# Due times of attention in a fused attention and two-MLP kernel: a weight conversion step moved behind an evacuation, and other places moved by tenths

## The chip, the cores and the metric

The kernel runs on one core of a Trainium2 chip. The metric is the device time of one execution in microseconds, the median of several runs. Engines are called as the profile does: PE (TensorE), DVE (VectorE), ACT (ScalarE), POOL (GpSimd), SP (SyncE, which issues the DMAs).

## The reference, cut to what matters

Attention over 2 x 8 heads, 768 positions and 64 features per head, with a mask from locality-sensitive hashing; then an MLP with a sigmoid gate; then an MLP with a quadratic activation.

```python
def _attn_ref(q, k, v, proj):
    q_bits = (np.einsum('bhsd,dk->bhsk', q, proj) > 0).astype(np.int64)
    ...
    mask = q_bucket[:, :, :, None] == k_bucket[:, :, None, :]
    scores = scale * np.matmul(q, k.transpose(0, 1, 3, 2))
    scores = np.where(mask, scores, -1000000000.0)
    scores = scores - np.max(scores, axis=-1, keepdims=True)
    attn = np.exp(scores)
    attn = attn / (np.sum(attn, axis=-1, keepdims=True) + 1e-09)
    return np.matmul(attn, v).astype(np.float32)

def _moe_ref(x, w_gate, w_val, w_out):
    gate = 1.0 / (1.0 + np.exp(-(x @ w_gate)))
    val = x @ w_val
    return (gate * val @ w_out).astype(np.float32)

def _moe2_ref(x, w_in, w_out):
    h = x @ w_in
    g = np.where(h >= 1.0, h, np.where(h <= -1.0, 0.0, (h + 1.0) ** 2 / 4.0))
    return (g @ w_out).astype(np.float32)
```

The MLP weights come as 64-bit floats; 1536 tokens of 512 features pass through both MLPs.

## The kernel before

**Attention** works on eight pairs of heads, numbered 0 to 7 by the loop variable q. A pair has twelve units (six blocks of 128 rows for each of the two heads). For a unit, TensorE makes the scores (QK, line 597) in one of two PSUM score buffers, VectorE takes the row maximum (MAX, 605), ScalarE the exponential with its row sum (EXP, 609). The results are transposed in eighteen groups of 512 columns for each pair: TensorE transposes (T, 631), ScalarE writes a scaled half-precision copy (HI, 640), VectorE the rest that the copy lost (LO, 643); three PSUM banks (p0, p1, mm) serve the transposes in the order in which they come free. Three products with the values follow in each pair (PV, 709), all in one PSUM bank with the tag "pv" and one buffer, each cut into three runs of twelve steps. VectorE evacuates a product with one instruction (EV, line 718), which multiplies it with the inverse row sums. Those arrive over GpSimd (RB, 890), TensorE (R, 875) and ScalarE (RS, 879). In this text T 7.17 is the transpose with index 17 of pair 7, and E7.1 is the evacuation with index 1 of pair 7, that of attention's last but one product; E7.2 is the last one.

**Weights.** The MLP weights are 64-bit floats, which the kernel takes apart into 32-bit words and rebuilds as 32-bit floats: the absolute value of the high words (a_abs, ScalarE, 164), the largest one over both halves (a_max, VectorE, 265 and 267), then a_conv in six steps: clamping (step 0, GpSimd, 167), a shift (1, VectorE, 170), the low words of half 0 and half 1 (2 and 3, line 173), and the sign of half 0 and half 1 (4 and 5, line 176). Four sums of quarters follow (a_sum, line 334; the first adds two quarters of half 1), since the first MLP's products are made by a scheme with fewer multiplications (the products a, b, c, d, e of class Quad), and scaled copies and rests (a_hi 342, a_lo 350). The scale comes from the row of maxima (row_in, 239 to 249) over a DMA. "g0" and "v0" are the first chunks of gate and value weights, "g1" the next chunk of gate weights; a chunk's two raw buffers are loaded on SyncE's queue (a_load, 309 to 312) when an older chunk's conversion has left them.

**What sets the order.** Every operation of attention has a due time: 12 times the pair, plus a number from a table (AT for the first and last pair, AM for those between, F0 for special steps of pair 0). The list of operations is sorted by due time and written out in that order (line 1030), so that a number in a table decides only what stands before what on each engine's queue. The conversion of v0 is placed by line 1024, the g0 steps by line 977. The program of the MLPs is a second list of that kind (line 1581), and some of its instructions stand, in the queues, between the last ones of attention. Lines 1032 to 1048, without due times, finish attention and the first gate product. The second MLP ends with strips of products (class Quad2), whose first strip takes its places from PA[0].

Of the kernel before, what the change touches and what calls it, by code (L numbers as in the profile page):

```python
# [23 lines left out]
EXP = 0x7F800000  # L24
# [12 lines left out]
def lsh_attention_glu_act(ctx, tc, qt, kt, v, proj, w_gate, w_val, w_out1, w_in2, w_out2, ident_d, code_d, out):  # L37
# [435 lines left out]
    with ExitStack() as actx:  # L473
# [246 lines left out]
        NAT, PR, VR, VS, RS, PT, STS = {}, {}, {}, {}, {}, {}, {}  # L720
# [7 lines left out]
        with tc.manual_schedule():  # L728
# [54 lines left out]
            for dst, r in ((3, E), (2, O)):  # L783
# [8 lines left out]
            F0 = {  # L792
                "max": (0.835, 4.3363, 4.8113, 6.0),
                "first": (1.1116, 1.92, 2.6321, 2.6521),
# [5 lines left out]
                "MAX": (-0.86, 0.21, 0.88, 1.91, 2.7, 4.3082, 4.6882, 5.3482, 7.3656, 9.7482, 9.8482, 8.9617),  # L800
                "EXP": (0.22, 0.6565, 1.1565, 2.5865, 2.8165, 4.4, 4.86, 7.05, 8.14, 10.5074, 11.21, 9.27),
# [9 lines left out]
                "BITS": (3.6634,),  # L811
# [13 lines left out]
            AM = {  # L825
                "QK": (-1.6212, -0.312, 0.1234, 1.0922, 0.2911, 4.4841, 2.6311, 3.1388, 4.9681, 7.5662, 8.3203, 9.8239),
                "MAX": (-0.8384, -0.282, 0.274, 2.0221, 1.7029, 4.7833, 2.832, 3.457, 5.7284, 8.6318, 8.8402, 9.9223),
                "EXP": (-0.0169, 0.1389, 0.7054, 2.7327, 1.7202, 5.1256, 3.1579, 4.9368, 7.4948, 9.0696, 9.801, 10.9635),
# [17 lines left out]
                "V4": (8.2939,),  # L846
                "RB": (7.5895, 9.9185, 12.8309),
                "VR": (7.1203,),
                "VT": (10.3243,),
                "STP": (6.1912, 6.7323, 11.461),  # L850
            }
# [8 lines left out]
            def at(kind, i, q, fn, *args):  # L860
                prog.append((UP * q + (tab(q)[kind][i] if isinstance(kind, str) else kind), len(prog), fn, args))
# [43 lines left out]
            for q in range(NQ):  # L905
# [46 lines left out]
                if q + 1 < NQ:  # L952
                    T = tab(q)
# [22 lines left out]
            for i in range(13):  # L976
                q, t = ((1, 1.3756), (1, 2.5756), (1, 5.1058), (2, 2.7058), (2, 3.9058), (2, 5.1058), (2, 6.3058), (3, 2.9841), (3, 7.7841), (4, 2.7841), (4, 4.7739), (4, 5.3408), (4, 6.0))[i]
                at(t, 0, q, next, fw, None)
            last = NQ - 1
# [41 lines left out]
            for i in range(2):  # L1021
                at(11.9 + 0.65 * i, 0, last, a_abs, "v0", i)
                at(10.8628 + 0.7012 * i, 0, last, a_max, "v0", i)
            for i, t in enumerate((13.0012, 13.3012, 13.6012, 13.4, 13.85, 14.0)):
                at(t, 0, last, a_conv, "v0", i)
# [391 lines left out]
    for m in range(2):  # L1417
# [3 lines left out]
        "g": {"seed": (0.4974, 2.358, 4.976), "p5": 3.5377, "sum": (3.99, 5.128, 7.1683, 8.1683), "act": (5.4565, 7.5607, 8.0579, 7.094)},  # L1421
        "v": {"seed": (0.3623, 2.8959, 5.4602), "p5": 2.4313, "sum": (3.0782, 5.7535, 7.5389, 6.9122), "act": (3.7144, 5.3665, 5.5617, 6.5916)},
    }
# [5 lines left out]
    for k in range(1, 2 * NT):  # L1429
        s0, T = 7 * k, QP[name(k // 2)[0]]  # L1430
# [8 lines left out]
    for t in range(2, NT):  # L1439
        base, n = 14 * (t - 1), name(t)  # L1440
        T = WP[n if n in WP else n[0]]
# [102 lines left out]
    ZA = [z_at((1.5403, 2), (3.2361, 2), (6.5761, 4), (11.2361, 2), (13.0358, 2)), z_at((1.3658, 2), (4.6958, 4), (9.3658, 3), (14.1405, 3))]  # L1544
    PA = [(2.33, -0.4877, 4.1823, 5.0776, 8.8423, 9.8423, 12.67), (1.0, -1.7115, 3.33, 4.306, 8.0, 9.0, 12.0)]
    SA = [(3.367, 8.2105, 11.95), (2.01, 6.95, 10.6)]
    CA = [{"a": (6.3682, 7.0823, 7.5823, 8.7823, 10.1657), "b": (10.8729, 11.3823, 11.9323, 13.0675, 13.3852), "c": (12.5147, 12.9147, 12.9295, 15.0221, 16.7088), "d": (13.55, 14.2829, 14.8829, 15.4829, 15.5329)},
          {"a": (5.34, 5.8, 6.3, 7.4, 7.9), "b": (9.6, 10.5884, 10.9383, 12.2, 12.8), "c": (11.1, 11.6, 12.2, 12.75, 13.8127), "d": (13.9575, 14.4775, 14.9497, 15.4997, 15.9997)}]
    for w in range(F2H + 1):
# [5 lines left out]
        if w == F2H:  # L1555
            break
        for i, d in enumerate(PA[m]):
            on(t0 + d, m_op, w, "P", i)
# [3 lines left out]
        for i, g in ((4, "b"), (5, "c")):  # L1562
            on(t0 + PA[m][i] + 1.0537, m_op, w, "add", g)
        for g, ds in CA[m].items():
# [64 lines left out]
```

## Time and profile before

| | us |
| --- | --- |
| median of 3 runs | 761.7 |
| lowest, highest run | 761.12, 762.7 |
| profiled execution | 759.33 |
| its span, first to last instruction | 757.5 |

Lengths and starts in the rows below belong to the profiled execution, counted from the start of its span. Attention takes up about the first 240 us of it. In a timeline, a row gives the start, the length, the engine, the source line, the operation, what it writes and reads, and in brackets the idle time before it with the operation that ended it. Several instructions of a kind that follow one another are one row (x2, x12).

### The profile page before, as it was taken

To read this page: it belongs to the slowest core of one execution; us is meant where nothing else is said; L and a number is where in the kernel's file an instruction comes from. 1 tells how busy PE (TensorE), PEld (TensorE's weight loads), DVE (VectorE), ACT (ScalarE), POOL (GpSimd) and SP (SyncE) were. 2 spreads that over 40 slices of the span, in tenths; PEclk is the share of its full clock that TensorE was granted. 3 is DMA by queue.
4 is the path that set the end of the run, shared out by engine and by line. 5 is a ranking of instruction groups with operands and counts; after the bars stand their busy time and mean duration, and the time that the engine had idled before them with its cause. 6 is when DMAs were issued, how large, how long until landed. Compare 5 with 4: busy or idle time off the path is not lost.

```text
span 757.5 us, 13220 instructions
## 1 busy us (share of the span) xinstructions
PE 728.7 (96%) x4883; PEld 461.5 (61%) x4883; DVE 648.1 (86%) x1141; ACT 521.1 (69%) x985; POOL 227.5 (30%) x311
## 2 busy tenths in 40 slices
PE   7899999999998999998999999998999999999997
PEld 4778878888885555555555556664555555555553
DVE  6899999889888989998889999999999996766643
ACT  6789889988885674673764445546776677767753
POOL 6435267774685653463430001103000000000000
PEclk9999999999999999999999999999999999999999
DMA  8564554454302155556565913533333200100002
GB/s 253 157 184 113 137 146 121 106 128 100 100 1 56 57 180 197 178 170 209 180 230 199 406 56 112 168 112 113 110 112 94 73 1 29 57 0 1 1 1 83
DMA packets 53200, 89.59 MB, mean 118 GB/s; under 512 B 9872, under 2 KB 33040, under 8 KB 53136
## 3 DMA queue, kind: packets, MB, share of 16 engines
q1 hardware_dynamic: 52400, 88.07, 37.8%
q8 instruction: 38, 0.62, 0.3%
q10 hardware_dynamic: 736, 0.69, 0.3%
q14 instruction: 26, 0.21, 0.1%
HBM read 68.65 MB, written 3.15 MB: 95 GB/s over the span
## 4 chain that ended last, share of the span: by engine, by line
PE 35%; DVE 22%; DMA 4%; ACT 3%; issue 2%; POOL 1%; SPq 1%; ACTq 0%; DVEq 0%; POOLq 0%
DVE h L131 2%; PE p L423 2%; PE p L422 2%; PE p L421 2%; DMA gi<-in_moe_w_in_dram 2%; PE qa L1357 2%; DVE gmx L209 2%; PE qa L1356 2%; PE qa L1355 2%; PE qe L1356 2%; PE qe L1355 2%; PE qe L1357 2%; PE o L1356 2%; PE o L1357 2%; PE o L1355 2%; DVE h L392 2%
## 5 line engine op out<-in xcount | busy, mean ns | idle before, releaser
L643 DVE SCALAR_TENSOR_TENSOR PT<-pt,PT 128x512 f16<-128x512 f32 x144 | 95.2, 681 | 8.5 <-ACT PT L640 7.0
L605 DVE TENSOR_REDUCE st<-sc 128x1 f32<-128x768 f32 x96 | 90.7, 948 | 6.5 <-PE sc L597 5.5
L609 ACT ACTIVATE P<-sc,st 128x768 f32<-128x768 f32 x96 | 87.1, 908 | 8.7 <-DVE st L605 7.9
L640 ACT ACTIVATE PT<-pt 128x512 f16<-128x512 f32 x144 | 82.2, 599 | 11.4 <-PE pt L631 9.7
L631 PE MATMUL pt<-ident,P 128*128 128x128 f32 x576 | 80.9, 279 | 0.8 <-DVE PT L643 0.5
L631 PEld LDWEIGHTS pt<-ident,P 128*128 128x128 f32 x576 | 65.4, 142 | 13.7 <-issue 8.8
L709 PE MATMUL O<-PT,vh 128*64 128x256 f16 x576 | 54.4, 277 | 2.1 <-DVE xr L718 2.1
L421 PE MATMUL p<-y,i 128*128 128x384 f16 x128 | 41.7, 326 | 0.0
L422 PE MATMUL p<-y,i 128*128 128x384 f16 x128 | 41.7, 326 | 0.0
L423 PE MATMUL p<-y,i 128*128 128x384 f16 x128 | 41.7, 326 | 0.0
L709 PEld LDWEIGHTS <-vh 128*64 128x64 f16 x576 | 31.0, 109 | 15.1 <-issue 14.6
L1357 PEld LDWEIGHTS <-g 128*128 128x128 f16 x192 | 18.9, 98 | 25.1 <-DVE g L131 2.3
L709 PE MATMUL O<-PT,vl 128*64 128x256 f16 x288 | 33.8, 273 | 0.0
L242 POOL TENSOR_SCALAR row<-row 1x1 uint32<-1x1 uint32 x15 | 5.5, 369 | 91.0 <-DVE row L240 90.9
L597 PE MATMUL sc<-N,N 128*128 128x384 f32 x96 | 29.3, 386 | 3.1 <-ACT N L533 1.9
L1334 ACT ACTIVATE t<-p,usc 128x384 f32<-128x384 f32 x32 | 21.3, 665 | 15.9 <-PE p L423 15.8
L1355 PEld LDWEIGHTS <-g 128*128 128x128 f16 x192 | 18.9, 98 | 21.3 <-ACT g L1344 1.3
L421 PE MATMUL y<-h,w_o 128*128 128x384 f16 x96 | 31.3, 326 | 0.4 <-DVE h L392 0.4
L1356 PEld LDWEIGHTS <-g 128*128 128x128 f16 x192 | 18.9, 98 | 20.5 <-issue 0.8
L423 PE MATMUL y<-h,w_o 128*128 128x384 f16 x96 | 31.3, 326 | 0.0
L422 PE MATMUL y<-h,w_o 128*128 128x384 f16 x96 | 31.3, 326 | 0.0
L597 PE MATMUL sc<-H,H 128*128 128x384 f32 x96 | 28.9, 382 | 2.3 <-ACT P L609 2.2
(355 smaller groups left out, 2292.8 us busy)
## 6 DMA issues: line engine op xcount, KB each, us to landing
wr_o<-in_moe_w_out_dram SPq DMA_DIRECT2D x28, 512.0 KB, 4.6
gi<-in_moe_w_in_dram SPq DMA_DIRECT2D x21, 384.0 KB, 4.8
gz<-in_moe_w_out_dram SPq DMA_DIRECT2D x21, 384.0 KB, 7.5
go<-in_moe_w_out_dram SPq DMA_DIRECT2D x16, 384.0 KB, 4.6
H<-U SPq DMA_DIRECT2D x28, 192.0 KB, 3.3
wr_i<-in_moe_w_in_dram SPq DMA_DIRECT2D x8, 512.0 KB, 3.8
wr_i<-in_moe_w_in_dram SPq DMA_DIRECT2D x16, 256.0 KB, 3.0
n<-in_qt_dram SPq DMA_DIRECT2D x8, 384.0 KB, 4.3
```

Of the source, the lines that this page charges most:

```text
L421: nc.tensor.matmul(ps, lhsT=wh, rhs=rh, start=first, stop=False, **kw)
L422: nc.tensor.matmul(ps, lhsT=wh, rhs=rl, start=False, stop=False, **kw)
L423: nc.tensor.matmul(ps, lhsT=wl, rhs=rh, start=False, stop=last, **kw)
L605: nc.vector.tensor_reduce(out=self.st[:, 0, self.c:self.c + 1], in_=self.sc[:, :, 0:HN], op=ALU.max, axis=AX.XY, negate=True)
L609: nc.scalar.activation(out=self.P, in_=self.sc[:, :, 0:HN], func=AF.Exp, bias=self.st[:, 0, self.c:self.c + 1], scale=1.0, accum_out=self. ...
L631: nc.tensor.transpose(self.ps[m][:, j, :], un[2 * self.n + e].P[:, a, c:c + 128], ident)
L640: nc.scalar.activation(out=self.part(0, m), in_=self.ps[m], func=AF.Copy, scale=PSCALE)
L643: nc.vector.scalar_tensor_tensor(out=self.part(1, m), in0=self.ps[m], scalar=PSCALE, in1=self.part(0, m), op0=ALU.mult, op1=ALU.subtract)
L709: nc.tensor.matmul(O_ps[r, 0:GN], lhsT=vv[m][:, e, i * D:(i + 1) * D], rhs=PT[:, l, e * NI + i, :], start=(s == 0), stop=(s == len(steps) ...
L1355: nc.tensor.matmul(OA[b][i], lhsT=gh[:, ts], rhs=wh, start=(fc == ORD2[0]), stop=False)
L1356: nc.tensor.matmul(OA[b][i], lhsT=gh[:, ts], rhs=wl, start=False, stop=False)
L1357: nc.tensor.matmul(OA[b][i], lhsT=gl[:, ts], rhs=wh, start=False, stop=(fc == ORD2[-1]))
```

## The change

Only numbers of the due-time tables change. By them:

- The six steps of a_conv for v0 get new places (line 1024): step 3 moves behind LO 7.17, step 2 with it, step 4 keeps its place ahead of E7.1, and step 5 (the sign of half 1) goes behind E7.1 and the step after it.
- E7.1 and the evacuation with index 1 of pair 0 get a later number, and so does the run 7.2.0 of products, which keeps its place.
- The g0 steps (line 977) move: the two maxima later in pair 1, the last sign step ahead of a maximum in pair 3, two scaled copies ahead of exponentials in pair 4.
- HI x.1 goes ahead of EXP x.6 in pairs 1 to 6. Scores 0.5 go ahead of the bit matmuls of pair 1, T 0.15 ahead of scores 1.2, scores 1.8 ahead of product run 0.2.0.
- On GpSimd the row-sum steps (RB, ST) of some pairs stand one or more instructions earlier; in pair 3 one stands three later. The start of the exponents of the second batch (two VectorE steps) goes ahead of one LO and one MAX.
- The PSUM banks p0 and mm of the transposes change places from T 0.17 on.
- In the second MLP, product 2 of the first strip goes behind product 3.

```diff
             F0 = {
-                "max": (0.835, 4.3363, 4.8113, 6.0),
+                "max": (0.6194, 4.3363, 4.8113, 6.0),
...
             AT = {
...
-                "EXP": (0.22, 0.6565, 1.1565, 2.5865, 2.8165, 4.4, 4.86, 7.05, 8.14, 10.5074, 11.21, 9.27),
-                "T": (1.0239, 2.59, 3.35, 4.67, 2.61, 5.43, 4.79, 5.11, 6.21, 8.68, 8.94, 9.7526, 9.188, 11.2, 10.61, 12.1511, 12.24, 12.67),
+                "EXP": (0.22, 0.6565, 1.1565, 2.5865, 2.8165, 4.4, 4.86, 6.3485, 8.14, 10.5074, 11.21, 9.27),
+                "T": (1.0239, 2.59, 3.35, 4.67, 2.61, 5.43, 4.79, 5.11, 6.21, 8.68, 8.94, 9.7526, 9.188, 11.2, 10.6815, 12.004, 12.24, 12.67),
...
-                "LO": (2.21, 3.0, 4.389, 4.86, 3.39, 6.35, 5.341, 7.902, 9.5625, 9.1416, 9.72, 10.51, 9.86, 11.85, 11.54, 12.52, 12.78, 13.76),
+                "LO": (2.21, 3.0, 4.389, 4.86, 3.39, 6.35, 5.341, 7.902, 9.5625, 9.1416, 9.72, 10.51, 9.86, 11.85, 11.54, 12.5975, 12.8575, 13.8375),
...
-                "PV": (8.9762, 9.9662, 10.1088, 11.7462, 12.3362, 13.8003, 16.8262, 17.52, 19.68),
-                "EV": (10.5468, 16.46, 20.5),
-                "Z": (2.95,),
+                "PV": (8.9762, 9.9662, 10.1088, 11.7462, 12.3362, 13.8003, 17.0773, 17.52, 19.68),
+                "EV": (10.5468, 16.8975, 20.5),
+                "Z": (3.178,),
...
             AM = {
-                "QK": (-1.6212, -0.312, 0.1234, 1.0922, 0.2911, ...),
+                "QK": (-1.6212, -0.312, 0.1234, 1.0809, 0.2911, ...),
...
-                "EXP": (-0.0169, 0.1389, 0.7054, 2.7327, 1.7202, 5.1256, 3.1579, 4.9368, ...),
+                "EXP": (-0.0169, 0.1389, 0.7054, 2.7327, 1.7202, 5.1256, 3.1579, 4.6699, ...),
...
-                "HI": (1.0934, 3.2326, 3.0876, 4.3999, ...),
+                "HI": (1.0105, 3.1497, 3.0047, 4.3999, ...),
...
-                "RB": (7.5895, 9.9185, 12.8309),
-                "VR": (7.1203,),
-                "VT": (10.3243,),
-                "STP": (6.1912, 6.7323, 11.461),
+                "RB": (7.5895, 8.88, 11.7924),
+                "VR": (6.0818,),
+                "VT": (9.2858,),
+                "STP": (5.1527, 6.7323, 11.461),
...
             for i in range(13):
-                q, t = ((1, 1.3756), (1, 2.5756), (1, 5.1058), ..., (3, 2.9841), (3, 7.7841), (4, 2.7841), (4, 4.7739), (4, 5.3408), (4, 6.0))[i]
+                q, t = ((1, 2.1099), (1, 3.3099), (1, 5.8401), ..., (3, 2.7429), (3, 7.5429), (4, 2.5429), (4, 4.5327), (4, 5.0996), (4, 5.7589))[i]
...
             for i in range(2):
-                at(11.9 + 0.65 * i, 0, last, a_abs, "v0", i)
+                at(11.6588 + 0.65 * i, 0, last, a_abs, "v0", i)
...
-            for i, t in enumerate((13.0012, 13.3012, 13.6012, 13.4, 13.85, 14.0)):
+            for i, t in enumerate((12.9754, 13.2754, 14.0754, 13.8742, 16.8242, 17.0000)):
                 at(t, 0, last, a_conv, "v0", i)
...
-        "v": {"seed": (0.3623, 2.8959, 5.4602), ...
+        "v": {"seed": (0.3623, 2.8959, 5.4765), ...
...
-    PA = [(2.33, -0.4877, 4.1823, 5.0776, 8.8423, 9.8423, 12.67), ...
+    PA = [(2.33, -0.4877, 5.0948, 5.0776, 8.8423, 9.8423, 12.67), ...
```

## Rows read from the trace of the kernel before

**Rows 1.** Page, part 1: busy us (share) and instructions by engine.

```profile
PE 728.7 (96%) x4883; PEld 461.5 (61%) x4883; DVE 648.1 (86%) x1141; ACT 521.1 (69%) x985; POOL 227.5 (30%) x311
```

**Rows 2.** Windows: length, busy us of PE, PEld, DVE, ACT, POOL; PEclk, DMA.

```profile
125.00:150.00 25.00, 25.00 (x240) 20.92 (x233) 21.78 (x34) 23.43 (x49) 20.19 (x23) 1.00 0.50 128
...
220.00:240.00 20.00, 17.79 (x182) 13.21 (x181) 18.36 (x32) 11.80 (x24) 15.30 (x19) 1.00 0.18 51
```

**Rows 3.** Timeline of TensorE: start, us, operation, [idle before, its releaser].

```profile
235.06 0.33 PE L423 MATMUL qa<-pB,a_g 128*128 128x384 f16 x1
237.49 0.30 PE L709 MATMUL O<-PT,vh 128*64 128x256 f16 x2 [2.11 <-DVE xr L718]
...
239.58 0.34 PE L421 MATMUL qb<-pT,s_g 128*128 128x384 f16 x1
```

**Rows 4.** Timeline of ScalarE, the same stretch and later.

```profile
234.93 0.38 ACT L879 ACTIVATE rs<-r 128x256 f32<-128x256 f32 x1 [0.50 <-PE r L875]
237.47 0.51 ACT L153 CAST pB<-xr 128x384 f16<-128x384 f32 x1 [2.16 <-DVE xr L718]
...
247.45 0.93 ACT L342 ACTIVATE a_v<-wt_v,wsc 128x768 f16<-128x768 f32 x1
```

**Rows 5.** Timeline of VectorE at the end of attention.

```profile
230.79 2.09 DVE L173 SCALAR_TENSOR_TENSOR wt_v<-wr_v,wt_v 128x512 uint32<-128x512 uint32 x2
232.81 0.68 DVE L643 SCALAR_TENSOR_TENSOR PT<-pt,PT 128x512 f16<-128x512 f32 x1
233.41 2.78 DVE L176 SCALAR_TENSOR_TENSOR wt_v<-wr_v,wt_v 128x512 uint32<-128x512 uint32 x2
...
236.22 0.42 DVE L334 TENSOR_TENSOR ws_v<-wt_v 128x256 f32<-128x256 f32 x1
...
237.02 0.42 DVE L718 SCALAR_TENSOR_TENSOR xr<-O,rs 128x256 f32<-128x256 f32 x1
...
239.69 0.42 DVE L718 SCALAR_TENSOR_TENSOR xr<-O,rs 128x256 f32<-128x256 f32 x1 [1.11 <-PE O L709]
...
241.85 0.56 DVE L131 TENSOR_TENSOR pT<-xt,pT 128x384 f16<-128x384 f32 x1 [0.68 <-ACT pT L153]
```

**Rows 6.** Timeline of GpSimd, the same stretch.

```profile
234.20 1.44 POOL L131 TENSOR_TENSOR xt<-xr,xt 128x384 f32<-128x384 f32 x1
...
244.41 0.50 POOL L153 CAST pB<-xr 128x384 f16<-128x384 f32 x1 [7.00 <-ACT qb L386]
```

**Rows 7.** Timeline of VectorE, sign steps of later weights.

```profile
254.43 1.27 DVE L176 SCALAR_TENSOR_TENSOR wt_g<-wr_g,wt_g 128x512 uint32<-128x512 uint32 x2
```

**Rows 8.** Timeline of TensorE, its next wait.

```profile
249.42 0.34 PE L421 MATMUL qd<-pT,a_g 128*128 128x384 f16 x1 [0.66 <-ACT qd L386]
```

**Rows 9.** Timeline of SyncE's queue: the load of the next gate weights' half 1.

```profile
236.26 0.37 SPq L311 DMA_DIRECT2D wr_g<-in_moe_w_gate_dram  x1
```

**Rows 10.** Timelines of VectorE and TensorE in pair 1.

```profile
49.84 0.89 DVE L267 TENSOR_TENSOR wsc<-wsc 128x1 f32<-128x1 f32 x1
...
52.74 0.62 PE L597 MATMUL sc<-N,N 128*128 128x384 f32 x2 [1.03 <-ACT P L609]
```

**Rows 11.** Timelines of VectorE and TensorE in pair 3.

```profile
103.97 1.75 DVE L176 SCALAR_TENSOR_TENSOR wt_g<-wr_g,wt_g 128x512 uint32<-128x512 uint32 x1
...
107.93 0.63 PE L631 MATMUL pt<-ident,P 128*128 128x128 f32 x4 [0.54 <-DVE PT L643]
```

**Rows 12.** Timeline of ScalarE in pair 2.

```profile
77.36 0.90 ACT L609 ACTIVATE P<-sc,st 128x768 f32<-128x768 f32 x1 [0.58 <-DVE st L605]
...
78.25 1.07 ACT L640 ACTIVATE PT<-pt 128x512 f16<-128x512 f32 x2
```

**Rows 13.** Timeline of ScalarE in pair 4.

```profile
130.17 0.83 ACT L342 ACTIVATE a_g<-wt_g 128x768 f16<-128x768 f32 x1
```

**Rows 14.** Timeline of ScalarE in the second MLP's first strip.

```profile
636.03 0.47 ACT L1280 ACTIVATE mc_m<-mb_m 128x384 f32<-128x384 f32 x1 [0.68 <-DVE ta_m L1304]
```

**Rows 15.** Window of the lowered clock: columns as in rows 2.

```profile
25.20:28.60 3.40, 3.40 (x13) 3.30 (x14) 2.78 (x4) 1.34 (x4) 0.23 (x1) 0.50 0.75 192
```

More of the change, by code (lines that the diff above doesn't have):

```diff
@@ L825, in lsh_attention_glu_act @@
             AM = {
-                "QK": (-1.6212, -0.312, 0.1234, 1.0922, 0.2911, 4.4841, 2.6311, 3.1388, 4.9681, 7.5662, 8.3203, 9.8239),
+                "QK": (-1.6212, -0.312, 0.1234, 1.0809, 0.2911, 4.4841, 2.6311, 3.1388, 4.9681, 7.5662, 8.3203, 9.8239),
                 "MAX": (-0.8384, -0.282, 0.274, 2.0221, 1.7029, 4.7833, 2.832, 3.457, 5.7284, 8.6318, 8.8402, 9.9223),
-                "EXP": (-0.0169, 0.1389, 0.7054, 2.7327, 1.7202, 5.1256, 3.1579, 4.9368, 7.4948, 9.0696, 9.801, 10.9635),
+                "EXP": (-0.0169, 0.1389, 0.7054, 2.7327, 1.7202, 5.1256, 3.1579, 4.6699, 7.4948, 9.0696, 9.801, 10.9635),
                 "T": (0.6726, 2.7818, 2.4903, 2.8259, 5.6069, 4.8189, 4.5978, 6.1506, 6.3992, 8.0591, 8.0212, 8.3198, 10.1114, 11.2138, 10.6646, 10.8685, 12.1144, 12.284),
[1 row of a table removed]
[1 row of a table added]
                 "LO": (2.054, 4.2198, 3.2826, 5.2606, 7.9391, 5.7821, 5.4721, 7.5402, 7.967, 9.0285, 8.7977, 9.5983, 10.7969, 12.174, 11.1739, 12.0774, 12.8392, 13.9848),
@@ L976, in lsh_attention_glu_act @@
             for i in range(13):
-                q, t = ((1, 1.3756), (1, 2.5756), (1, 5.1058), (2, 2.7058), (2, 3.9058), (2, 5.1058), (2, 6.3058), (3, 2.9841), (3, 7.7841), (4, 2.7841), (4, 4.7739), (4, 5.3408), (4, 6.0))[i]
+                q, t = ((1, 2.1099), (1, 3.3099), (1, 5.8401), (2, 2.7058), (2, 3.9058), (2, 5.1058), (2, 6.3058), (3, 2.7429), (3, 7.5429), (4, 2.5429), (4, 4.5327), (4, 5.0996), (4, 5.7589))[i]
                 at(t, 0, q, next, fw, None)
@@ L1421, in lsh_attention_glu_act @@
         "g": {"seed": (0.4974, 2.358, 4.976), "p5": 3.5377, "sum": (3.99, 5.128, 7.1683, 8.1683), "act": (5.4565, 7.5607, 8.0579, 7.094)},
-        "v": {"seed": (0.3623, 2.8959, 5.4602), "p5": 2.4313, "sum": (3.0782, 5.7535, 7.5389, 6.9122), "act": (3.7144, 5.3665, 5.5617, 6.5916)},
+        "v": {"seed": (0.3623, 2.8959, 5.4765), "p5": 2.4313, "sum": (3.0782, 5.7535, 7.5389, 6.9122), "act": (3.7144, 5.3665, 5.5617, 6.5916)},
     }
@@ L1544, in lsh_attention_glu_act @@
     ZA = [z_at((1.5403, 2), (3.2361, 2), (6.5761, 4), (11.2361, 2), (13.0358, 2)), z_at((1.3658, 2), (4.6958, 4), (9.3658, 3), (14.1405, 3))]
-    PA = [(2.33, -0.4877, 4.1823, 5.0776, 8.8423, 9.8423, 12.67), (1.0, -1.7115, 3.33, 4.306, 8.0, 9.0, 12.0)]
+    PA = [(2.33, -0.4877, 5.0948, 5.0776, 8.8423, 9.8423, 12.67), (1.0, -1.7115, 3.33, 4.306, 8.0, 9.0, 12.0)]
     SA = [(3.367, 8.2105, 11.95), (2.01, 6.95, 10.6)]
```

2 rows, old and new, of the table AM are left out of this document.

## The prediction

> **What bounds the kernel now.** I read the page first: TensorE is busy for 728.7 us, 96% of the span [rows 1], so a change pays where TensorE stands still or in the chain that makes it stand still. The windows by stage come next: 2.2 of 20 us of TensorE are free between 220 and 240 us, the end of attention, against none between 125 and 150 us, attention's middle [rows 2]. TensorE's timeline there shows one large hole: after 235.06 nothing starts until 237.49, 2.11 us put down to the evacuation on line 718 [rows 3]. I call the places pair.index, as the tables count: T/HI/LO 7.17 is the last transpose of the last pair with its ScalarE copy and its VectorE rest, E7.1 the evacuation of the last but one product.
>
> VectorE's timeline shows why E7.1 is late. Its other operand, the ScalarE copy on line 879, starts at 234.93 and takes 0.38, so it is there at 235.31 [rows 4]. VectorE is not free then: it does both sign steps of the value weights (line 176, from 233.41, 2.78 us for the two), a step of the exponent row and two of the four weight sums (line 334, from 236.22), and only at 237.02 E7.1 (0.42 us) [rows 5]. Of the next product TensorE can start nothing before, since both products use one PSUM bank ("pv", one buffer).
>
> **The change, part by part.** I sorted the due times before and after for every engine.
>
> *The end of attention.* VectorE's order was: shift (line 170), low words half 1 and 0 (173), LO 7.17, sign half 0, sign half 1 (176), E7.1, one b21 remainder (131), last evacuation E7.2. It becomes: shift, LO 7.17, the low words, sign half 0, E7.1, the remainder, sign half 1, E7.2. Of the six steps only the last passes E7.1: sign half 0 is due at 16.8242, E7.1 at 16.8975. But a sum needs both signed halves (the first reads two quarters of half 1), so the four sums follow half 1.
>
> When can E7.1 start? The low words began at 230.79; LO 7.17 (0.68) now goes first, then the two low words (2.09) and one sign step (half of 2.78, 1.39) [rows 5]: 230.79 + 0.68 + 2.09 + 1.39 = 234.95. That is before the other operand, 235.31, so that is late next: E7.1 at about 235.37, done at 235.79, and TensorE's next product at 235.84 in place of 237.49: **1.65 us earlier**. Bounds: 2.1, if nothing is left of the hole, and 0.9, if both low words and the sign step cost 0.75 more.
>
> What is queued behind: in the old order VectorE was idle for 1.11 us ahead of E7.2 [rows 5]. Now the remainder waits for the cast of E7.1's result (0.51, [rows 4]), then some 0.5 of its own (the same operation has 0.56 at 241.85, a little of it overlapped, [rows 5]), then the sign step, then sums. The product takes from 237.49 to 239.58 [rows 3], so E7.2 could start 2.2 us after TensorE's restart, at 238.05. The remainder ends at 235.79 + 0.55 + 0.5 = 236.85. A sign step costs 1.39 here, where GpSimd works beside it (a two-input operation of 1.44 from 234.20 on, [rows 6]), and 0.64 later (1.27 for two at 254.43, [rows 7]); GpSimd is idle for 7.00 us before 244.41 [rows 6], so I take 0.64: 237.5. Two sums (0.42 at 236.22, and the next operation starts a little before one ends, so 0.36 each) fill the time to 238.2, E7.2 is some 0.2 late against the ideal. The other two sums cost 0.7, and 0.68 of VectorE's idle time before 241.85 (waiting for a ScalarE cast) takes most of it [rows 5]. So of the 1.65 the VectorE-ScalarE chain behind E7.2 keeps about 1.35. Does this or TensorE's own 1.65 decide? TensorE's next wait of any size is 0.66 at 249.42, and it is for ScalarE [rows 8], which works through its queue behind VectorE's results: so the chain decides. **Term: -1.35** (bounds -0.6, with four sums and a sign step of 1.39 before E7.2, and -1.65).
>
> The Trainium skill, "SBUF — State Buffer", section "Who interferes with whom", says that a VectorE instruction with two SBUF inputs and a GpSimd instruction that reads SBUF exclude each other, and that the later one waits out the whole of the earlier. By that rule the second sign step, which ended at 236.19, waited for the GpSimd operation that ended at 235.64, and moved behind E7.1 it costs 0.64; with the other reading, 1.39 wherever it stands, E7.2 would be 0.75 later and the term -0.6.
>
> The weight load of the second gate's half 1 waits until half 1's raw buffer is free, that is until the sign step is done: it is issued at some 237.6 where it was at 236.26 [rows 9], and behind it on SyncE's queue stands the broadcast of the value weights' scale. Its users, ScalarE's scaled copies from 247.45 on [rows 4], are some 10 us off. Cost nothing; without that cover, 1.3.
>
> *Pair 1.* The first gate weights' maxima (line 265) and combination (267) move: the first from before MAX 1.4 to behind LO 1.0, the second and the combination from before MAX 1.6 to behind LO 1.2. Now MAX 1.6 comes right behind the combination (0.89 at 49.84), EXP 1.6 needs it, and TensorE waits 1.03 at 52.74 for EXP 1.6 [rows 10]. MAX 1.6 can come up to 0.9 earlier. But maximum and combination then stand before MAX 1.7, and VectorE gets no less work. I take -0.2 (bounds -0.9, all of it kept, and +0.3, what MAX 1.7 loses if the next scores are as tight). A transpose ahead of scores 1.2, the scores 0.5 ahead of the bit matmuls, scores 1.8 ahead of a product: each goes into a wait of at most 0.3; inside that bound.
>
> *Pair 3.* The last sign step of the gate weights goes ahead of MAX 3.6. Behind it it took 1.75 at 103.97, and TensorE then waited 0.54 at 107.93 for VectorE [rows 11]. MAX 3.6 was waiting for its scores, so part of the step now fills that wait: -0.3, between nothing and the 0.54.
>
> *Pairs 1 to 6.* HI x.1 goes ahead of EXP x.6. In pairs 2, 3, 5 and 6 EXP x.6 waited 0.48 to 0.58 for its maximum (pair 2's row: 0.58 at 77.36), the length of a copy (1.07 for two, [rows 12]): nothing. In pair 4 two copies of gate weights (0.83 at 130.17, [rows 13], and one of two thirds its columns) go ahead of EXP 4.3 and 4.5; scores 4.7 and the code matmuls wait for these PSUM buffers, by my count 0.15 each past the old times: +0.3 (0 to +1.4, both copies in full).
>
> *The rest.* Row-sum broadcasts and two row steps move on GpSimd and SyncE past work due 9 or more scores later; buffer names of two PSUM banks swap. In the second MLP one product of the first strip goes behind the next, which frees its sum for ScalarE earlier (a copy waited 0.68 at 636.03, [rows 14]) but leaves TensorE's order full: 0 (-0.2 to +0.2).
>
> **Sum:** -1.35 - 0.2 - 0.3 + 0.3 = -1.55, taken as -1.6. The profiled execution took 759.33 (span 757.5 and 1.8 around), 0.3% under the median of the runs, 761.7; I carry the difference over: 757.7 for an execution like it and **760.1** for the median.
>
> **The rivals.** (a) *The sums crowd in*: the framework puts instructions of the next program into waits (two sums stand ahead of E7.1 now), so all four and a slow sign step may come before E7.2. Then -0.6 - 0.2 = -0.8: 760.9. For it: the present order. Against: GpSimd is idle. (b) *Nothing at E7.1*: the queue's real order isn't the due times' alone, and E7.1 stays at 237.0; -0.2 stays: 761.5. Against: everything in attention's own program stands in due order in VectorE's timeline. (c) *Slower*: the copies ahead of EXP x.6 aren't covered. If transpose x.1 ends later than the maximum, each of six pairs loses a copy of 0.5, and pair 4 its two, 1.4: 3.0 + 1.4 = 4.4, less 1.35, +3.05: 764.7. It decides once the pairs lose more than 1.35 + 1.5. For it: TensorE has no free time in the middle pairs [rows 2], so it loses at once. Against: the waits of EXP x.6 for the maximum [rows 12]. (d) *The clock*: in this execution TensorE's granted clock is 0.50, its lower level of 1.2 GHz, from 25.2 to 28.6 us [rows 15], after it had waited twice. Scores 0.5 move just ahead of that. If this stretch of 3.4 us goes away, half of it is saved: -1.7 more, 758.4; if it lengthens, the same the other way.
>
> **How the numbers follow.** Forecast 0.50, (a) 0.22, (b) 0.12, (c) 0.09, (d) 0.07. 0.2% is 1.5 us, about what a measurement of this kernel can tell from no change. Four fifths of the forecast's half lie above it: faster 0.40 + 0.07 = 0.47; same 0.10 + 0.22 + 0.12 = 0.44; slower 0.09. The range runs from 758.9 (every early term at its good end) to 761.9 (nothing at E7.1, the early terms together at +0.2) and leaves out (c), (d) and a little. The forecast's own range is 759.3 to 760.5.
>
> **What would show it.** Right: E7.1 at about 235.4, before the second line 176; that one at 0.6 to 0.7 us; TensorE's hole at 0.4 to 0.5; the wait at 249.42 no longer than 0.7. Wrong: E7.2 less than 1.2 us earlier, while TensorE restarts 1.65 earlier; new waits of TensorE in pairs 2 to 6; the line 879 copy itself moving.

## The result, and the profile after

The changed kernel took 756.09 us (median of 5 runs, 753.94 to 757.83), the kernel before beside it 762.7 (5 runs, 761.12 to 764.0): ratio 0.9915, 95% interval 0.9887 to 0.9943, or 6.5 us less (4.3 to 8.6). Forecast were 1.6 us less and a range down to 758.9. Two later comparisons gave 0.9932 (0.9908 to 0.9956) and 0.9946 (0.9925 to 0.9966). The direction was right, the size too small.

The page of the changed kernel's profiled execution (753.94 us), against [rows 1]:

```profile
span 752.2 us, 13229 instructions
...
PE 726.4 (97%) x4883; PEld 460.0 (61%) x4883; DVE 646.3 (86%) x1141; ACT 521.2 (69%) x985; POOL 228.0 (30%) x311
```

TensorE's busy time fell by 2.3 us; the rest of the 5.4 us by which this execution is shorter (759.33 to 753.94) is time in which TensorE stood still. TensorE's timeline at the end of attention:

```profile
232.76 0.33 PE L423 MATMUL qa<-pB,a_g 128*128 128x384 f16 x1
233.01 0.30 PE L709 MATMUL O<-PT,vh 128*64 128x256 f16 x2
...
235.10 0.34 PE L421 MATMUL qb<-pT,s_g 128*128 128x384 f16 x1
...
245.29 0.34 PE L421 MATMUL qd<-pT,a_g 128*128 128x384 f16 x1 [0.67 <-ACT qd L386]
```

The hole of 2.11 us [rows 3] is gone: the product starts as soon as the gate matmuls are done. VectorE's timeline, the same stretch:

```profile
231.17 1.20 DVE L176 SCALAR_TENSOR_TENSOR wt_v<-wr_v,wt_v 128x512 uint32<-128x512 uint32 x1
...
232.36 0.40 DVE L718 SCALAR_TENSOR_TENSOR xr<-O,rs 128x256 f32<-128x256 f32 x1
...
233.93 0.69 DVE L176 SCALAR_TENSOR_TENSOR wt_v<-wr_v,wt_v 128x512 uint32<-128x512 uint32 x1
234.65 0.42 DVE L334 TENSOR_TENSOR ws_v<-wt_v 128x256 f32<-128x256 f32 x1
...
236.12 0.42 DVE L718 SCALAR_TENSOR_TENSOR xr<-O,rs 128x256 f32<-128x256 f32 x1
...
237.71 0.56 DVE L131 TENSOR_TENSOR pT<-xt,pT 128x384 f16<-128x384 f32 x1
```

And ScalarE's:

```profile
232.63 0.38 ACT L879 ACTIVATE rs<-r 128x256 f32<-128x256 f32 x1 [0.50 <-PE r L875]
```

E7.1 starts at 232.36, before the line 879 copy at 232.63. So that copy is not E7.1's operand; it belongs to E7.2. The second sign step follows behind E7.1 at 0.69 us, and all four sums stand ahead of E7.2.

**By stages.** TensorE's transposing matmuls (line 631) give the cuts: numbers 73, 145, 217 and so on begin a pair's worth of 72. The table has the length of stages in us, from TensorE's timeline of one execution of each kernel; what the names from e1_end on stand for is told with the experiments. "Pair 1" runs from matmul 73 to 145, "2 and 3" from there to 289, "pair 4" to 361, "end" from the last transposing matmul to the last of the products.

```
kernel                        pair 1  2 and 3  pair 4   end
before, profiled              26.46   53.99    26.37   10.12
before, again (e16_before)    26.46   53.98    26.35   10.12
changed, profiled             26.01   52.71    26.56    7.94
changed, again (e5_after)     26.01   52.74    26.56    7.94
changed, again (e13_after)    26.00   52.70    26.56    7.94
e1_end                        26.45   54.00    26.38    7.94
e2_g0                         26.15   53.48    26.56   10.12
e3_am                         26.37   53.48    26.28   10.12
e4_early                      26.45   54.00    26.36   10.12
e7_rb                         26.48   53.48    26.36   10.12
e8_hi                         26.35   53.96    26.28   10.11
e14_no_end                    26.15   52.70    26.56   10.12
e11_sign_back                 26.00   52.70    26.56   10.01
e12_both_signs                26.01   52.74    26.74    7.94
e6_best                       26.00   52.70    26.28    7.94
e9_abs_g                      26.00   52.73    26.28    7.94
e10_abs_gv                    26.01   52.71    26.28    7.94
e15_best_signs                26.01   52.73    26.28    7.94
```

One order gives one length, to 0.04 us (pair 4 of e12_both_signs, 0.18 longer, is the exception; pairs 2 and 3 stand together because the kernel before has 0.4 more in the one and less in the other in its profiled execution). The stretch ahead of pair 1, some 45 us with the first loads, is left out, because it scatters: 44.5 to 46.1 in the eleven traces with e4_early's numbers for the first pair (45.46 on average) and 45.4 to 46.9 in the seven without (45.95). Half a microsecond between the averages, beside a standard deviation of 0.5 in each group, is too little to call shown. The change's parts are -0.45, -1.27, +0.20 and -2.18; of the last, 0.35 is given back just behind (the first gate matmuls come 4.48 us earlier than in [rows 3], 239.58 to 235.10, but the wait at 245.29 ends only 4.13 earlier than in [rows 8]). Sum: **-3.35 us** in attention.

The same traces can be cut behind attention too, by TensorE's first matmuls into four tiles: y (the first MLP's output product), p (the second MLP's first product), me_m and md_m (products of its first strip).

- From attention's last product to y, the first MLP: 170.8 to 174.3 us in the eight traces that have the kernel before or one part of the change (172.1 on average), 171.0 to 177.8 in the eight that have all or most of it (173.6; e9_abs_g and e10_abs_gv, which change the first MLP, are left out).
- From y to p: 94.85 to 94.88 in all 18.
- From p to me_m: 120.15 or 120.16 in e3_am, e16_before, e10_abs_gv and e14_no_end, whose granted clock is 1.00 between 500 and 530 us, and 121.2 to 121.5 in the others, where it is 0.94. Both orders are in both groups.
- From me_m to md_m: 12.58 with the old place of product 2 and 12.54 with the new. That part of the change is worth 0.04.
- From md_m to the last matmul: 112.43 or 112.44 in all 18.

So behind attention the change shows as 0.04; the rest of the difference between executions there is the clock's and the first MLP's, and the first MLP is no shorter with the change.

### The profile page after: what moved, and what is told of

The parts are those of the page before. It is cut to its first block, busy times and chain, and to the rows that moved or that the text cites. A ratio compares the mean times of both kernels' runs of the same rounds, so it can differ in the third digit from the quotient of the medians.

```text
span 752.2 us, 13229 instructions
## 1 busy us (share of the span) xinstructions
PE 726.4 (97%) x4883; PEld 460.0 (61%) x4883; DVE 646.3 (86%) x1141; ACT 521.2 (69%) x985; POOL 228.0 (30%) x311
## 4 chain that ended last, share of the span: by engine, by line
PE 36%; DVE 22%; DMA 4%; ACT 3%; issue 2%; POOL 1%; SPq 1%; ACTq 0%; DVEq 0%; POOLq 0%
PE p L421 2%; PE p L423 2%; PE p L422 2%; DVE h L131 2%; DMA gi<-in_moe_w_in_dram 2%; DVE gmx L209 2%; PE qa L1357 2%; PE qa L1356 2%; PE qa L1355 2%; PE qe L1356 2%; PE qe L1355 2%; PE qe L1357 2%; PE o L1357 2%; PE o L1356 2%; PE o L1355 2%
```

## The experiments

**The four parts of the change alone.** e1_end takes lines 804, 808, 809, 1022 and 1024; e2_g0 line 977; e3_am lines 826, 828, 830 and 847 to 850 (table AM); e4_early lines 793, 801, 802 and 810. Two numbers of the change are in none of them: the seed of the value products in the first MLP (5.4602 to 5.4765), which no run has alone, and PA[0], whose 0.04 is told above. Of each the core:

```diff
 e1_end
-                "EV": (10.5468, 16.46, 20.5),
+                "EV": (10.5468, 16.8975, 20.5),
-            for i, t in enumerate((13.0012, 13.3012, 13.6012, 13.4, 13.85, 14.0)):
+            for i, t in enumerate((12.9754, 13.2754, 14.0754, 13.8742, 16.8242, 17.0000)):
 e2_g0
-... (1, 1.3756), (1, 2.5756), (1, 5.1058), ..., (3, 2.9841), (3, 7.7841), (4, 2.7841) ...
+... (1, 2.1099), (1, 3.3099), (1, 5.8401), ..., (3, 2.7429), (3, 7.5429), (4, 2.5429) ...
 e3_am
-                "HI": (1.0934, 3.2326, 3.0876,
+                "HI": (1.0105, 3.1497, 3.0047,
-                "RB": (7.5895, 9.9185, 12.8309),
+                "RB": (7.5895, 8.88, 11.7924),
 e4_early
-                "Z": (2.95,),
+                "Z": (3.178,),
```

> The kernel before with the edits of the end of attention alone (value weight steps, E7.1, products, rests of transposes, and with them one score block behind a product in pair 0/1). Theory A (place by place, read from the two traces: TensorE 2.18 earlier at 237 us, 0.33 given back by 245): -1.8 us against before, E7.1 right behind its product, hole of 2.11 gone, all four sums ahead of E7.2. Rival B (the end gives only what the prediction had, 1.35, and the rest of the change's 5.4 came from execution-to-execution differences): -1.3. Rival C (the whole change of the median, 6.6, hangs on the end): -6.

> The kernel before with line 977 alone (places of the gate weight steps in pairs 1, 3 and 4). Theory A: pair 1 -0.4 and pair 3 -0.9 on TensorE's line (0.5 and 1.1 in the whole change, some of it the copies' places), pair 4 0 to +0.2: -1.2 in all; the sign step ahead of MAX 3.6 takes 1.2 us in place of 1.75, and TensorE's wait of 0.54 at 107.9 is gone. Rival (the predicted term): -0.2 - 0.3 + 0.3 = -0.2.

> The kernel before with the edits of the middle pairs' table alone (copies HI x.1 ahead of EXP x.6, row-sum broadcasts ahead of GpSimd's rests, steps of g0 and v1 around them). Theory A: the wait of 0.17 at 94.57 in pair 3 and the 0.4 that TensorE lost there are gone, pair 4 gives 0.2 back: -0.2 to -0.4, between nothing and -0.5. Rival (c) of the prediction, uncovered copies: +3.

> The kernel before with the edits of the first pair's tables alone (scores 0.5 ahead of the bit matmuls, a transpose ahead of scores 1.2). Theory A (the granted clock of 0.50 between 25.2 and 28.6 us depends on the order there): the stretch is gone, and the run is 0.7 shorter on TensorE's line by 32 us (0.6 lost before 12 us by chance, 1.3 gained). Rival (the stretch comes and goes between executions of the same kernel): no difference, 0 +- 0.5, and the stretch is in some execution's trace whatever the order.

Ratios to the kernel before: 0.9977 (0.9958 to 0.9997), 1.0005 (0.9982 to 1.0029), 0.9980 (0.9957 to 1.0003), 0.9978 (0.9952 to 1.0004), from 12 runs each beside 35 of the kernel before, which spread from 755.73 to 764.5. An interval of 0.4% is wider than three of the four effects, so the stages decide. The end alone gives all of 2.18, less 0.34 behind it, as theory A had it; rivals B and C fall. The g0 steps give 0.31 in pair 1, 0.50 in 2 and 3, and take 0.2 in pair 4: 0.6 in all, half of what theory A expected, and the sign step takes 1.92, not 1.2. Table AM gives 0.5 in pairs 2 and 3, where the prediction had nothing, and 0.1 each in pairs 1 and 4: 0.7, more than theory A's 0.5 at most. The first pair's tables alone change no stage of the table, and what they do ahead of pair 1 is lost in the scatter there.

**What in table AM.** e7_rb takes only lines 847 to 850 (GpSimd's row-sum broadcasts RB x.11 ahead of rest0, and the reductions and row steps), e8_hi only 826, 828 and 830 (copies HI x.1 ahead of EXP x.6).

```diff
 e7_rb
-                "RB": (7.5895, 9.9185, 12.8309),
+                "RB": (7.5895, 8.88, 11.7924),
 e8_hi
-                "HI": (1.0934, 3.2326, 3.0876,
+                "HI": (1.0105, 3.1497, 3.0047,
```

> The kernel before with the row-sum broadcasts, row steps of the last values and GpSimd reductions of the middle pairs' table alone. In the run with the whole table the last sign step of the gate weights took 1.64 us at 102.92, against 2.16 in a run that keeps this stretch as it was, and TensorE's wait at 107 was 0.41 against 0.90. Theory A (GpSimd's order decides how long the sign step takes beside it): all of that comes here: the sign step 1.64, the wait 0.4. Rival (the copies HI x.1 ahead of EXP x.6 give it): sign step 2.16 and wait 0.9, as before.

> The kernel before with the copies HI x.1 ahead of EXP x.6 alone (and scores 1.3 by a hundredth, which moves nothing). Theory A: nothing, 0 +- 0.1 in every pair, with the sign step at 2.16 and the wait of 0.90 at 107 as before. Rival: the gain of 0.5 in pair 3 is here. Rival (c) of the prediction: +0.5 in each of six pairs.

TensorE's wait in pair 3, from its timeline, in e7_rb:

```profile
106.91 0.63 PE L631 MATMUL pt<-ident,P 128*128 128x128 f32 x4 [0.41 <-DVE PT L643]
```

and in e8_hi:

```profile
108.55 0.63 PE L631 MATMUL pt<-ident,P 128*128 128x128 f32 x4 [0.89 <-DVE PT L643]
```

All of it comes with GpSimd's order, none with the copies; the copies cost nothing in any pair (at most 0.1 gained in pairs 1 and 4). Rival (c) of the prediction is out. Why a broadcast of 0.40 us on GpSimd moves TensorE is seen in the timeline of both engines at the last sign step of the gate weights: what GpSimd does when the step starts, and the step. The kernel before, again:

```profile
103.56 1.66 POOL L131 TENSOR_TENSOR pT<-xT,pT 128x768 f16<-128x768 f32 x1
...
103.63 2.13 DVE L176 SCALAR_TENSOR_TENSOR wt_g<-wr_g,wt_g 128x512 uint32<-128x512 uint32 x1
```

e7_rb, with the broadcast some 8 us ahead of the step:

```profile
94.94 0.40 POOL L890 COPY rb<-st 128x256 f32<-128x256 f32 x1 [1.15 <-DVE st L615]
...
102.33 1.83 POOL L506 TENSOR_TENSOR W<-n,U 128x768 fp32r<-128x768 f32 x1
...
103.06 1.64 DVE L176 SCALAR_TENSOR_TENSOR wt_g<-wr_g,wt_g 128x512 uint32<-128x512 uint32 x1
```

e2_g0:

```profile
100.86 1.85 POOL L506 TENSOR_TENSOR W<-n,U 128x768 fp32r<-128x768 f32 x1
...
101.34 1.92 DVE L176 SCALAR_TENSOR_TENSOR wt_g<-wr_g,wt_g 128x512 uint32<-128x512 uint32 x1
```

The changed kernel:

```profile
100.83 0.83 POOL L693 CAST vh<-vr 128x768 f16<-128x768 f32 x1
...
101.00 1.20 DVE L176 SCALAR_TENSOR_TENSOR wt_g<-wr_g,wt_g 128x512 uint32<-128x512 uint32 x1
...
101.62 2.27 POOL L506 TENSOR_TENSOR W<-n,U 128x768 fp32r<-128x768 f32 x1
```

GpSimd's operation ends at 105.22, 104.16, 102.71 and (the cast) 101.66; the sign step ends at 105.76, 104.70, 103.26 and 102.20: 0.54 or 0.55 later each time. So the step's recorded length holds a wait for the GpSimd operation that was under way at its start, and its own work is what follows: most of the 0.69 that it takes with no such neighbour. It works the other way too: in the changed kernel the step came first, and GpSimd's next operation took 2.27 in place of 1.83 to 1.85. The Trainium skill, "SBUF — State Buffer", section "Who interferes with whom", says that these two engines share a port pair, that this pair is an exclusive lock, that a VectorE instruction with two SBUF inputs contends for it with a GpSimd instruction that reads SBUF, and that the order of issue decides who waits. The traces agree in all four, by the 0.54. In this execution of the kernel before the step starts 0.07 after an operation of 1.66 and waits nearly all of it out. The broadcast, put ahead of rest0, makes GpSimd wait 1.15 us for VectorE's reciprocal (line 615), so that all of GpSimd's work behind it comes some 1.1 us later against the step; and moving the step ahead of MAX 3.6 sets it beside an earlier operation, in the changed kernel a short cast. Each alone gives 0.5, both together 1.27, and TensorE's waits say why. The kernel before, again, and e2_g0:

```profile
107.97 0.63 PE L631 MATMUL pt<-ident,P 128*128 128x128 f32 x4 [0.90 <-DVE PT L643]
```

```profile
105.20 0.62 PE L597 MATMUL sc<-N,N 128*128 128x384 f32 x2 [0.40 <-ACT P L609]
```

e7_rb shortens the wait of 0.90 to 0.41. e2_g0 removes it, but the sign step of 1.92 now stands ahead of MAX 3.6, and TensorE waits 0.40 for the exponential behind that maximum. In the changed kernel the step takes 1.20 there, and neither wait is left.

Pair 1 holds the same wait, but its gain comes from elsewhere. In [rows 10] the combination (line 267) takes 0.89 at 49.84, and GpSimd's timeline of the kernel before says why:

```profile
48.87 1.84 POOL L506 TENSOR_TENSOR W<-n,U 128x768 fp32r<-128x768 f32 x1
```

That ends at 50.71, the combination at 50.73. In the changed kernel the combination stands later, with GpSimd idle beside it:

```profile
51.22 0.16 DVE L267 TENSOR_TENSOR wsc<-wsc 128x1 f32<-128x1 f32 x1
```

0.16 in place of 0.89. TensorE's wait of 1.03 [rows 10] is 0.66, but a new one of 0.35 stands behind it (1.75 us later), on VectorE: 1.01 together, so these waits gave nothing back. The gain stands ahead of them. Line 977 moves more than the maxima: the same step makes ScalarE's absolute value of that half (line 164) and then the maximum. ScalarE's timeline, TensorE's weight loads (PEld) and its matmuls in the kernel before:

```profile
47.37 0.72 ACT L164 ACTIVATE wt_g<-wr_g 128x512 f32<-128x512 f32 x1
47.98 0.90 ACT L609 ACTIVATE P<-sc,st 128x768 f32<-128x768 f32 x1
...
49.03 0.30 PEld L597 LDWEIGHTS sc<-H,H 128*128 128x128 f32 x2 [0.21 <-ACT P L609]
...
50.74 0.62 PE L597 MATMUL sc<-N,N 128*128 128x384 f32 x2
```

and in the changed kernel:

```profile
46.61 0.89 ACT L609 ACTIVATE P<-sc,st 128x768 f32<-128x768 f32 x1
...
47.49 0.69 ACT L164 ACTIVATE wt_g<-wr_g 128x512 f32<-128x512 f32 x1
...
48.03 0.30 PEld L597 LDWEIGHTS sc<-H,H 128*128 128x128 f32 x2
...
49.63 0.59 PE L597 MATMUL sc<-N,N 128*128 128x384 f32 x2
```

The absolute value stood ahead of an exponential for which the next scores waited, and now stands behind it. Counted from the start of pair 1's stage (46.18 and 45.42) the exponential comes 0.61 us earlier, the scores no longer wait for it, and the scores after them start 0.35 earlier (50.74 and 49.63), ahead of both waits. So the 0.31 of e2_g0 is put down to ScalarE's order by reading the traces; no run moves the absolute values without the maxima, and what the shorter combination saves beside that isn't shown. Nor do the parts add up here: e14_no_end (below), with all but the end's numbers, has e2_g0's 26.15, and the last 0.14 comes only together with these. They stand in table AT, which holds for pair 0 too; why they tell in pair 1 stays open.

**The end, one step at a time.** e11_sign_back puts the second sign step back ahead of E7.1; e12_both_signs puts both behind it.

```diff
 e11_sign_back, against the changed kernel
-... (12.9754, 13.2754, 14.0754, 13.8742, 16.8242, 17.0000)
+... (12.9754, 13.2754, 14.0754, 13.8742, 16.8242, 16.8250)
 e12_both_signs
-... (12.9754, 13.2754, 14.0754, 13.8742, 16.8242, 17.0000)
+... (12.9754, 13.2754, 14.0754, 13.8742, 16.9500, 17.0000)
```

> The changed kernel with one thing undone: the sign step of half 1 stands ahead of E7.1 again, behind that of half 0. The changed kernel has E7.1 at 232.36, right behind its product, and no hole. Theory A (the sign step is the price): E7.1 0.7 to 1.3 later, TensorE's hole 0.8 to 1.3 in place of none, and some sums ahead of E7.1 too would add 0.4 each, as in the kernel before. Rival (LO 7.17 ahead of the low words gave it): hole at most 0.3.

> The changed kernel with both sign steps behind E7.1. Theory A (E7.1 already starts as its product ends): TensorE no earlier by more than 0.1, and E7.2 no earlier, since both sign steps and four sums then stand ahead of it: E7.2 0 to 0.7 later, of which the chain behind keeps 0 to 0.3. Rival (VectorE still binds at E7.1): -0.5.

The timeline of VectorE and TensorE in e11_sign_back:

```profile
230.30 2.61 DVE L176 SCALAR_TENSOR_TENSOR wt_v<-wr_v,wt_v 128x512 uint32<-128x512 uint32 x2
...
232.94 0.42 DVE L334 TENSOR_TENSOR ws_v<-wt_v 128x256 f32<-128x256 f32 x1
...
233.74 0.42 DVE L718 SCALAR_TENSOR_TENSOR xr<-O,rs 128x256 f32<-128x256 f32 x1
...
234.22 0.30 PE L709 MATMUL O<-PT,vh 128*64 128x256 f16 x2 [2.00 <-DVE xr L718]
```

The hole is back, 2.00 of 2.11, with LO 7.17 still ahead of the low words. So the place of one sign step is nearly the whole gain, 2.07 of the stage's 2.18 (10.01 against 10.12 and 7.94): the step of 1.4 beside GpSimd, and the two sums (0.8) that its end lets through ahead of E7.1. In e12_both_signs, VectorE's timeline, E7.1 waits for its product:

```profile
232.27 0.42 DVE L718 SCALAR_TENSOR_TENSOR xr<-O,rs 128x256 f32<-128x256 f32 x1 [0.85 <-PE O L709]
...
236.05 0.42 DVE L718 SCALAR_TENSOR_TENSOR xr<-O,rs 128x256 f32<-128x256 f32 x1
```

The end stage stays 7.94: the changed kernel is already at what the product allows. E7.2 is no later (236.05 against 236.12, where 0 to 0.7 later was expected).

**The whole again, and its complement.** e5_after and e13_after are the changed kernel; e14_no_end is it with the lines of e1_end as before; e16_before is the kernel before.

> The changed kernel, unchanged, beside the kernel before on one chip. Theory A: in attention, which repeats to a few hundredths of a microsecond from trace to trace, the change saves 3.4 us (0.45 in pair 1, 1.3 in pairs 2 and 3, -0.2 in pair 4, 1.85 at the end); the rest of the first comparison's difference (6.6 of the medians, 5.4 of the traces) lies in waits for DMAs in the first MLP and in the granted clock, which vary as much between executions of one kernel: -3.4 here, between -2.5 and -4.5. Rival: the MLP part belongs to the change too (its loads start earlier or fall better): -5 to -7.

> The changed kernel again. Attention alone, by the stages that repeat to hundredths in all traces, gives 3.4; the two comparisons so far gave 6.5 +- 2.1 and 5.2 +- 1.8. Theory A (nothing but attention's 3.4): ratio 0.9955 +- 0.002 here. Rival (some 2 us more, outside attention, belong to the change): 0.993 +- 0.002.

> The changed kernel with the end of attention undone. By the stages: the holes of pairs 1 to 4 only, 1.5 to 1.7 us against before, ratio 0.998; the end stage as before, with the hole of 2.1. Together with the run of the end alone (0.9977) that would make 0.9957 for both. Rival (the two parts strengthen one another): the whole is at 0.993, more than the product.

> The kernel before, unchanged, in the place of a changed one: how far two sets of executions of one kernel lie apart. Ratio 1.000, interval to include it; and its trace shows whether the stretch at a granted clock of 0.50 between 25 and 29 us comes again (theory A: it doesn't, or elsewhere).

Ratios: e5_after 0.9932 (0.9908 to 0.9956, 6 runs), e13_after 0.9946 (0.9925 to 0.9966), e14_no_end 0.9964 (0.9938 to 0.9991), e16_before 1.0009 (0.9988 to 1.0030), the last three from 12 runs each beside another 35 of the kernel before. Attention's 3.35 is 0.9956 of 760. e13_after's interval holds it, and the rival's 0.993 too; e5_after's ends at it, and its 5.2 us lie in the rival's range and not in theory A's; that of the first comparison does not hold it. So the whole times lean to more than 3.35, by 0.7 to 3.1 us, while the stages show no place for it: behind attention only 0.04 is the change's, and the first MLP, in the traces, is no shorter. The parts e1_end and e14_no_end multiply to 0.9941, the whole to 0.9946: nothing points to a strengthening. By the stages e14_no_end saves 1.4, a little under the 1.5 to 1.7 expected. In e14_no_end TensorE's hole at the end is there as before:

```profile
235.74 0.30 PE L709 MATMUL O<-PT,vh 128*64 128x256 f16 x2 [2.11 <-DVE xr L718]
```

What scatters is the first MLP. The waits of ScalarE, and of TensorE behind it, between 240 and 380 us (total, times, longest), in the changed kernel's profiled execution:

```profile
ACT wt_g L164 <- DMA wr_g<-in_moe_w_gate_dram: 4.7, 5, 2.4
...
PE qb L421 <- ACT qb L386: 3.5, 4, 2.4
```

and in e5_after, the same kernel:

```profile
ACT wt_g L164 <- DMA wr_g<-in_moe_w_gate_dram: 7.1, 6, 2.2
...
PE qb L421 <- ACT qb L386: 5.6, 5, 2.2
```

2.1 us of difference in TensorE's waits between two executions of one kernel, behind the landing of weight loads. The clock scatters as well. Windows by stage (columns as in [rows 2]), e16_before, with the old order:

```profile
25.00:29.00 4.00, 3.72 (x16) 3.62 (x17) 3.31 (x6) 1.98 (x5) 0.40 (x1) 0.58 0.81 200
```

the changed kernel's profiled execution:

```profile
25.00:29.00 4.00, 2.99 (x20) 2.68 (x21) 3.39 (x8) 3.44 (x7) 0.40 (x1) 1.00 0.56 144
```

and e13_after, the same kernel:

```profile
25.00:29.00 4.00, 3.99 (x17) 3.86 (x17) 2.87 (x5) 2.16 (x5) 0.00 (x0) 0.57 0.65 166
```

The stretch at the lower level comes with either order and stays away with either (e1_end, with the old order there, has 1.00 in this window); e16's expectation that it would not come again there was wrong, and so was e4_early's theory A as a claim on the order.

**Three versions meant to be better.** e6_best is the changed kernel with the gate copies of pair 4 back in their old places; e15_best_signs is e6_best with the edit of e12_both_signs; e9_abs_g is e6_best with ScalarE's absolute values of the gate chunks (line 164) behind the copies on lines 389 and 386; e10_abs_gv does that for the value chunks too.

```diff
 e6_best, against the changed kernel (line 977)
-(4, 2.5429), (4, 4.5327), (4, 5.0996), (4, 5.7589)
+(4, 2.7841), (4, 4.7739), (4, 5.3408), (4, 6.0)
 e9_abs_g, against e6_best
-        "g": {"load": -12.353, "abs": (-7.6756, -6.6904),
+        "g": {"load": -12.353, "abs": (-6.4500, -6.4000),
 e10_abs_gv, against e9_abs_g
-"abs": (-6.6935, -4.8952), "conv": (-4.4301,
+"abs": (-6.6300, -4.1000), "conv": (-4.0900,
```

> The changed kernel with the scaled gate copies of pair 4 back behind EXP 4.3, 4.7 and 4.5. The changed kernel's pair 4 took 26.56 us on TensorE's line against 26.28 in the run with the middle pairs' table alone and 26.37 before. Theory A: 0.2 to 0.3 faster than the changed kernel in that stretch, all else the same. Rival (the copies were wanted early by GpSimd's remainders): no gain, or a loss of 0.3.

> The changed kernel with pair 4's gate copies back and both sign steps of the value weights behind E7.1. By the stages: 0.28 less in pair 4 than the changed kernel, nothing more at the end, so 0.3 faster than it, which a comparison of whole times can't show: ratio 0.9951 by theory A, 0.9925 by the rival of the run above.

> The kernel of the last comparison (the changed kernel with pair 4's gate copies back), and in the first MLP the two absolute values of each later chunk of gate weights (line 164, ScalarE) behind the copies on lines 389 and 386 that stood behind them. In all ten traces ScalarE waits 2.2 to 2.8 us at 353 to 358 for the landing of these weights, and TensorE stands still for some 2 us behind it. Theory A (the wait costs because finished products queue behind it on ScalarE): -2 us against that kernel, -5.5 to -6 against before, and TensorE's hole there at most 0.3. Rival (the weights themselves are late for their use): the hole moves to a later place, no gain.

> The same, and the absolute values of the value weights behind the copies of line 386 too, with the clamping step moved behind them. The waits there are 0.2 to 1.7 us at 340 to 345. Theory A: 0 to -1 against the run before, since there the copies wait less; and the times scatter less between executions. Rival: the value weights' conversion is then late for its scaled copies, +0.5.

e6_best gains 0.28 in pair 4 by the stages, as expected; its ratio, 0.9941 (0.9919 to 0.9962), can't show that beside the changed kernel's 0.9932 of the same comparison. e15_best_signs came out at 0.9965 (0.9944 to 0.9987). Both beat the kernel before; that either beats the changed kernel is shown for pair 4's stage alone. The interval of e15_best_signs holds theory A's 0.9951 and leaves out the 0.9925 by which something outside attention would belong to the change. e9_abs_g, 0.9967 (0.9949 to 0.9985), and e10_abs_gv, 1.0006 (0.9988 to 1.0024), gained nothing. For e9_abs_g the rival held; e10_abs_gv came out some 3 us above it, where its rival had 0.5, and why so much was not looked at. TensorE's waits between 240 and 380 us in e9_abs_g:

```profile
PE qa L423 <- DVE a_v L350: 2.8, 4, 0.9
PE qb L421 <- ACT qc L386: 1.9, 6, 1.1
...
PE qb L421 <- ACT qb L386: 0.3, 1, 0.3
```

The wait behind the loads is down to 0.3 (3.5 and 5.6 above), but TensorE now waits for the rests of the value weights (a_v, line 350) and for the copies of product c (qc, line 386) instead.

## Why the prediction was wrong in size

- **The end, -1.35: measured -1.83.** The mechanism was right: the sign step off E7.1's path, 0.69 us behind it. What failed is the answer to "when can E7.1 start". The line 879 copy at 234.93 was taken for E7.1's operand and so for what is late next; it is E7.2's. E7.1 waits for its product alone, so the whole hole went (the bound of 2.1, not 1.65; a hole of 0.4 to 0.5 was to be left). Behind E7.2 it came out much as the term had it, by another way: all four sums did crowd in ahead of E7.2, as rival (a) feared, and E7.2 came only 1.27 us earlier (236.12 for 239.69, less 2.30 that had been won by the last transpose), but the 0.68 of VectorE's idle time behind it [rows 5] took up the rest: the operation behind that idle time, at 241.85, is at 237.71, 1.84 earlier counted the same way.
- **"Row-sum broadcasts and two row steps move on GpSimd": put at nothing, and the largest miss in the mechanism.** Alone they give 0.50 in pairs 2 and 3. **Pair 3, -0.3:** the sign step ahead of MAX 3.6 gives 0.50 alone, inside its bound of 0.54; both together give 1.27. The failing step is that the 1.75 of the sign step was taken for its own length. It held a wait for GpSimd, so GpSimd's order set it. The prediction used that very rule for the sign step at the end, and not here.
- **Pair 1, -0.2: measured -0.45,** inside the bounds, but not for the reason given. MAX 1.6 was to come earlier past the combination's 0.89 and shorten the wait of 1.03; the waits of 0.66 and 0.35 in its place add up to as much. The gain that the traces show is that of the scores ahead of it, from ScalarE's absolute values, which the prediction didn't see moving. "VectorE gets no less work" was wrong too: the combination took 0.16 in its new place.
- **Pair 4, +0.3: measured +0.2. HI x.1 ahead of EXP x.6, 0: measured 0 to -0.1.** Right; rival (c) fell. The wait at 245.29 was to be at most 0.7 and is 0.67; the load of the gate weights behind the sign step was to be issued 1.3 us later and was, by 1.4, with no new wait behind it (SyncE's broadcast of the scale now goes ahead of it).
- **The clock, rival (d):** the stretch did vanish between the two profiled executions, which counts for some 0.7 of their 5.4, but by chance, not by the change.
- **The range.** Its low end, 758.9, put the early terms at their good ends and left the end of attention at -1.35 and GpSimd's moves at 0. The stages' sum of 3.35 makes 758.35 of the 761.7 that the prediction started from, and misses the range narrowly. Much of the rest is that start: 761.7 was the median of three runs, and the larger sets of the kernel before have medians of 759.2 to 760.9 (12 to 35 runs), while the changed kernel has 755.2 to 756.2 in all three sets. From 760.1, the median of 35, the stages' sum comes to 756.8, against 756.09. What the three ratios have beyond 3.35 stays unexplained. It may be scatter of the first MLP, and some of it may lie ahead of pair 1; no trace shows a stage that holds it.

## What to carry to other kernels

Before moving an instruction, compare its row with the same operation elsewhere in the trace: 0.89 against 0.16 and 1.75 against 0.69 say that the row is mostly a wait, and what it waits for stands in another engine's timeline at the same time. In this kernel GpSimd's order was a term in VectorE's lengths, and VectorE's in GpSimd's, also where neither waited for the other's result. When a due time moves, list everything that moves with it on every engine: here a step named for its maximum also held a ScalarE operation. And where executions scatter by more than the effect, cut the trace into stages: what repeats to hundredths can be added up, and the rest kept apart.

## What the runs showed that was not expected

An instruction on 128x1 elements waited 0.73 us for a GpSimd operation that it shares no data with (0.89 against 0.16). The landing of loads in the first MLP moves TensorE's waits by 2 us from one execution of a kernel to the next, through finished products that queue on ScalarE behind the weights. Putting the products ahead of the weights only moved the waits to other places.
